# Layer 2 of a fused convolution and two-layer MLP kernel starts after three chunks of layer 1 in place of two

## The chip, the cores and the metric

One core of a Trainium2 chip runs the whole kernel. The metric is the device time of one execution in microseconds (us), a median over several executions. The engines of the core work in parallel, each through its own queue in order: PE (TensorE, the matmuls; PEld is its loading of weights), DVE (VectorE), ACT (ScalarE), POOL (GpSimd), SP (SyncE, which only issues DMAs here).

## The reference

```python
w = softmax(weight_gen, axis=-1)                 # (2, 4096, 8 heads, 7 taps)
x1[b, s, h, g] = sum_k w[b, s, h, k] * xpad[b, s + k, h, g]   # 192 = 8 heads x 24, causal, 7 taps
x1 = x1.reshape(8192, 192)
x2 = (sigmoid(x1 @ w_gate) * (x1 @ w_val)) @ w_out       # layer 1, 192 -> 1536 -> 192
h  = x2 @ w_in
out = (h * cos(h)) @ w_out2                              # layer 2, 192 -> 2048 -> 192
```

The weights of both layers come as 64-bit floats and are decoded on the chip; the products are computed to more than one float32r by a split of each operand in a high and a low half.

## The kernel before, in words

The 8192 tokens are cut into 16 **chunks** of 512 tokens. For each chunk a **convolution** on DVE (7 multiplications by a tap, `tap`, of 128x768 elements, and sums of them) gives x1 with tokens on the partitions. PE transposes it (`transposes`, L335, tile `pt`) and ACT and DVE split it in high and low halves (`split_input`, L357 and L363), which makes the layer's input `xT`.

A **step** of a layer is one call of `hidden` (18 matmuls of 64x512, L413, into two of the four PSUM banks `ph`) and the work on its result. There are 12 steps in layer 1 of a chunk and 8 in layer 2. In layer 1 ACT takes the sigmoid (L515), DVE multiplies (L518, which frees the two banks), ACT and POOL make the halves `gh` (L556) and `gl` (L557), and PE makes 10 matmuls with them (`out_matmuls`, L432) some two steps later. A step of layer 2 has two such tiles, so 20 of these matmuls, and a cosine in place of the sigmoid. At the end of layer 1 of a chunk `finish1` adds up the sums on ACT and DVE (L441, L442) and makes the input of layer 2 with three instructions on POOL (L452 and twice L122). At the end of layer 2 `finish2` transposes the result back (L469, tile `pf`) and stores it.

The order of the segments is written out by hand. Before the change it is layer 1 of chunks 0 and 1, then layer 2 of chunk 0, layer 1 of chunk 2, layer 2 of chunk 1, layer 1 of chunk 3, and so on: `LEAD = 2` segments of layer 1 first. Each engine's order of work follows from the order in which the loop over `steps` writes it. Side work is put at named steps by the list `side` (a step from which it may come, a step at which it must, a cost; `do_side`): the softmax of a group of chunks, the taps of the next chunk, and the **decoding** of weights. Decoding one unit takes ACT (L110, L113, for the weights into layer 2 also L147), DVE (L115), ACT (L120) and POOL (L122 for a unit of `w_in`, twice L184 for a unit of an output matrix). The eight units of layer 2 (four of `w_in`, four of `w_out2`) are decoded while layer 1 of chunk 1 runs, at steps 1 + i * 11 // 8.

For chunks 0, 1 and 2 the seven products of the taps are not added on DVE. `conv_products` keeps them, and PE transposes all seven into the same PSUM tile, which adds them up there: 112 small matmuls in place of 16. From chunk 3 on `conv_ops` adds them on DVE (L309): 7 multiplications and 6 additions, and 16 transposes. The transposes of a chunk stand in the last step of the layer 1 segment before its own.

The input tiles live in three buffers: `xB` for every layer 1 but chunk 0's, `xA` and `xC` in turn for layer 2.

## Time and profile before

| | us |
|---|---|
| median of 3 executions (1251.09 to 1253.61) | 1252.81 |
| the profiled execution | 1251.61 |
| its span in the trace | 1249.8 |
| PE busy | 1219.4 (98%) |
| DVE busy | 902.1 (72%) |
| ACT busy | 792.8 (63%) |
| POOL busy | 713.0 (57%) |

A share of busy time is a mean over the whole span. The table of stretches shows where an engine is full: in a row, an engine whose busy time equals the length of the stretch never rests in it. A row of the timeline gives start and length of some instructions that stand together, and in brackets how long the engine sat idle before them and what ended that. Where one instruction of a kind takes longer than the others of its shape, it waited inside itself for something that the profile doesn't name.

### The profile page before, as it was taken

To read this page: it belongs to the slowest core of one execution; us is meant where nothing else is said; L and a number is where in the kernel's file an instruction comes from. 1 tells how busy PE (TensorE), PEld (TensorE's weight loads), DVE (VectorE), ACT (ScalarE), POOL (GpSimd) and SP (SyncE) were. 2 spreads that over 40 slices of the span, in tenths; PEclk is the share of its full clock that TensorE was granted. 3 is DMA by queue.
4 is the path that set the end of the run, shared out by engine and by line. 5 is a ranking of instruction groups with operands and counts; after the bars stand their busy time and mean duration, and the time that the engine had idled before them with its cause. 6 is when DMAs were issued, how large, how long until landed. Compare 5 with 4: busy or idle time off the path is not lost.

```text
span 1249.8 us, 26898 instructions
## 1 busy us (share of the span) xinstructions
PE 1219.4 (98%) x11056; PEld 1058.3 (85%) x11056; DVE 902.1 (72%) x1309; ACT 792.8 (63%) x1326; POOL 713.0 (57%) x531
## 2 busy tenths in 40 slices
PE   6889999999999999999999999999999999999997
PEld 5677988898898888888898888989889899888886
DVE  7967887777877676877667787775877767683585
ACT  6765856648475574857557485664847557484674
POOL 3958645647465474655637465463746546464563
PEclk8999999999999999999999999999999999999999
DMA  9902202121111211111121120112111121020010
GB/s 250 248 20 58 63 14 69 27 70 27 45 32 34 69 26 54 43 45 27 26 82 27 46 52 14 58 27 74 27 45 26 40 58 26 14 52 14 1 27 26
DMA packets 27403, 61.94 MB, mean 50 GB/s; under 512 B 2580, under 2 KB 7698, under 8 KB 27280
## 3 DMA queue, kind: packets, MB, share of 16 engines
q1 hardware_dynamic: 26368, 59.09, 17.5%
q8 instruction: 86, 1.41, 0.5%
q10 hardware_dynamic: 912, 1.13, 0.3%
q14 instruction: 37, 0.30, 0.1%
HBM read 30.33 MB, written 6.29 MB: 29 GB/s over the span
## 4 chain that ended last, share of the span: by engine, by line
PE 84%; DVE 1%; ACT 1%; issue 0%; DVEq 0%; ACTq 0%
PE ph L413 46%; PE po L432 36%; PE pf L469 1%; PE pt L335 1%; DVE wk L546 0%; ACT wk L542 0%; ACT gh L556 0%; DVE wk L529 0%; DVE wk L532 0%; DVE wk L518 0%; ACT va L441 0%; DVE wk L537 0%; DVE gl L557 0%; ACT wk L536 0%; DVE pr L283 0%
## 5 line engine op out<-in xcount | busy, mean ns | idle before, releaser
L557 POOL TENSOR_TENSOR gl<-wk,gh 128x512 fp32r<-128x512 f32 x446 | 607.0, 1367 | 498.5 <-ACT gh L556 381.3
L413 PE MATMUL ph<-xT,unit 64*128 64x512 f32 x5760 | 772.8, 390 | 8.5 <-DVE wk L518 4.6
L413 PEld LDWEIGHTS ph<-xT,unit 64*128 64x128 f32 x5760 | 617.9, 185 | 104.0 <-DVE wk L518 13.6
L432 PE MATMUL po<-gh,outu 64*128 64x512 f32 x2688 | 552.1, 390 | 2.2 <-ACT gh L556 1.8
L432 PE MATMUL po<-gl,outu 64*128 64x512 f32 x1792 | 467.7, 389 | 4.6 <-POOL gl L557 4.6
L556 ACT ACTIVATE gh<-wk 128x512 fp32r<-128x512 f32 (+1 forms) x450 | 283.1, 629 | 249.1 <-DVE wk L518 206.1
L432 PEld LDWEIGHTS po<-gh,outu 64*128 64x128 f32 x2688 | 405.5, 185 | 37.2 <-ACT gh L556 2.7
L432 PEld LDWEIGHTS po<-gl,outu 64*128 64x128 f32 x1792 | 315.7, 185 | 28.8 <-POOL gl L557 6.4
L518 DVE TENSOR_TENSOR wk<-ph,wk 128x512 f32<-128x512 f32 x192 | 131.7, 686 | 146.4 <-ACT wk L515 136.0
L546 DVE SCALAR_TENSOR_TENSOR wk<-ph,wk 128x512 f32<-128x512 f32 (+1 forms) x258 | 168.4, 687 | 42.5 <-ACT wk L542 42.5
L542 ACT ACTIVATE wk<-wk,sin_bias 128x512 f32<-128x512 f32 (+1 forms) x258 | 173.0, 714 | 19.4 <-DVE wk L532 8.8
L515 ACT ACTIVATE wk<-ph 128x512 f32<-128x512 f32 x192 | 113.6, 592 | 57.8 <-PE ph L413 56.9
L529 DVE TENSOR_SCALAR wk<-ph 128x512 f32<-128x512 f32 x129 | 88.0, 682 | 64.1 <-PE ph L413 62.3
L536 ACT ACTIVATE wk<-ph 128x512 int32<-128x512 f32 x129 | 75.5, 585 | 73.6 <-PE ph L413 73.0
L309 DVE TENSOR_TENSOR acc<-acc,pr 128x768 f32<-128x768 f32 x78 | 102.0, 1308 | 0.4
L283 DVE TENSOR_TENSOR pr<-xp,sm 128x768 f32<-128x768 f32 x84 | 96.0, 1144 | 0.0
L532 DVE SCALAR_TENSOR_TENSOR wk<-wk,ph 128x512 f32<-128x512 f32 x129 | 88.1, 683 | 4.4
L537 DVE TENSOR_TENSOR wk<-wk,ph 128x512 f32<-128x512 int32 x129 | 87.3, 677 | 0.0
L442 DVE TENSOR_TENSOR va<-po,va 128x512 f32<-128x512 f32 x32 | 22.0, 688 | 39.1 <-PE po L432 29.1
L363 DVE TENSOR_TENSOR xT<-pt,xT 64x256 fp32r<-64x256 f32 (+1 forms) x76 | 27.2, 413 | 21.5 <-ACT xT L357 21.3
L357 ACT ACTIVATE xT<-pt 64x256 fp32r<-64x256 f32 (+1 forms) x66 | 20.4, 378 | 21.5 <-PE pt L335 21.3
L122 POOL TENSOR_TENSOR unit<-wf,unit 128x768 fp32r<-128x768 f32 (+1 forms) x11 | 22.2, 2022 | 15.8 <-ACT unit L120 15.8
(61 smaller groups left out, 507.8 us busy)
## 6 DMA issues: line engine op xcount, KB each, us to landing
xT<-xT SPq DMA_DIRECT2D x90, 256.0 KB, 3.9
xp<-in_x_dram SPq DMA_DIRECT2D x13, 960.0 KB, 4.8
out_dram<-o SPq DMA_DIRECT2D x16, 384.0 KB, 2.3
rawo<-in_moe_w_out_dram SPq DMA_DIRECT2D x7, 768.0 KB, 15.9
raw<-in_moe_w_in_dram SPq DMA_DIRECT2D x8, 384.0 KB, 15.7
raw<-in_moe_w_gate_dram SPq DMA_DIRECT2D x5, 384.0 KB, 12.8
raw<-in_moe_w_val_dram SPq DMA_DIRECT2D x4, 384.0 KB, 15.3
sm<-in_weight_gen_dram SPq DMA_DIRECT2D x3, 336.0 KB, 5.1
```

Source lines behind the costliest of these rows:

```text
L283: nc.vector.tensor_tensor(out=out.rearrange("p t (h g) -> p t h g", g=G), in0=xp[c][:, k:k + TC, :].rearrange("p t (h g) -> p t h g", g=G) ...
L309: nc.vector.tensor_tensor(out=acc, in0=acc, in1=last, op=ALU.add)
L413: nc.tensor.matmul(ps[i], lhsT=u.t[r, w, (s + i) % NQ, c0:c0 + P], rhs=xt[r, x, s, :], start=n == 0, stop=n == len(terms) - 1,)
L432: nc.tensor.matmul(po[2 * i + a], lhsT=w[r, d0:d0 + P], rhs=g[r], start=first and g is gh and d0 < D, stop=last and g is gl,)
L515: nc.scalar.activation(out=self.w[0], in_=self.ps[0], func=AF.Sigmoid)
L518: nc.vector.tensor_tensor(out=self.w[0], in0=self.ps[1], in1=self.w[0], op=ALU.mult)
L529: nc.vector.tensor_scalar(out=w, in0=u, scalar1=0.25, scalar2=ROUND_MAGIC, op0=ALU.add, op1=ALU.add)
L532: nc.vector.scalar_tensor_tensor(out=w, in0=w, scalar=ROUND_MAGIC, in1=u, op0=ALU.subtract, op1=ALU.subtract)
L542: nc.scalar.activation(out=w, in_=w, func=AF.Sin, scale=-SIN_SCALE, bias=sin_bias)
L546: nc.vector.scalar_tensor_tensor(out=w, in0=self.ps[i][:, r], scalar=TWO_PI, in1=w, op0=ALU.mult, op1=ALU.mult)
L556: nc.scalar.activation(out=gh, in_=w, func=AF.Copy)
L557: eng.tensor_tensor(out=gl, in0=w, in1=gh.bitcast(F32), op=ALU.subtract)
```

## The change

- The segments become layer 1 of chunks 0, 1 and 2, then layer 2 of chunks 0 and 1, then layer 1 of chunk 3, layer 2 of chunk 2, layer 1 of chunk 4, and so on.
- Chunk 2 uses `conv_ops` as the later chunks do: its seven products are added on DVE, and PE transposes one tile.
- The eight units of layer 2's weights are decoded over layer 1 of chunks 1 and 2, at steps 1 + i * 22 // 8.
- The transposes and the split for chunk 3 move into step 5 of layer 2 of chunk 1, since no layer 1 segment stands right before chunk 3's own.
- The softmax group of chunks 3 to 5 becomes one of chunk 3 alone, loaded into the tile of the group before, and the groups of three start at chunk 4.
- The three input buffers take turns, for both layers.

```diff
-    groups = [(0, TC), (TC, 3 * TC)] + [(t0, min(t0 + GT, T)) for t0 in range(3 * TC, T, GT)]
+    groups = [(0, TC), (TC, 3 * TC), (3 * TC, 4 * TC)] + [(t0, min(t0 + GT, T)) for t0 in range(4 * TC, T, GT)]
...
+    HOME = {(1, 0): "xA", (1, 1): "xB", (1, 2): "xA", (2, 0): "xC", (2, 1): "xB", (2, 2): "xA"}
+
+    def input_tile(layer, c):
+
+        tag = HOME.get((layer, c)) or ("xC", "xB", "xA")[c % 3]
+        return tpool.tile([P, 2, NQ, N], F32R, name="xT", tag=tag)
...
-        big = tpool.tile([P, K - 3, TC, D], F32, name="prs", tag="xA" if c == LEAD else "xB")
+        big = tpool.tile([P, K - 3, TC, D], F32, name="prs", tag="xB")
...
-    LEAD = 2
-    segments = [(1, c) for c in range(LEAD)]
-    for c in range(NCH):
+    LEAD = 3
+    FINAL = 4
+    segments = [(1, c) for c in range(LEAD)] + [(2, 0)]
+    for c in range(1, NCH):
         segments.append((2, c))
-        if c + LEAD < NCH:
-            segments.append((1, c + LEAD))
+        if c + 2 < NCH:
+            segments.append((1, c + 2))
...
-        todo[n1:] = [(seg_start[1, 1] + 1 + i * (J1 - 1) // 8, u) for i, (_, u) in enumerate(todo[n1:])]
+        todo[n1:] = [(seg_start[1, 1] + 1 + i * (2 * J1 - 2) // 8, u) for i, (_, u) in enumerate(todo[n1:])]
...
-                a, b = [(seg_start[1, c - 3], seg_start[1, c - 2]), (k0, k0)][group_at[c] == 2]
+                a, b = [(seg_start[1, c - 3], seg_start[1, c - 2]), (k0, k0)][group_at[c] in (2, 3)]
                 if a == b:
+                    a += group_at[c] == 2
                     at = [a - 1] * 2 * n + [a] + [a + 1] * n + [a + 2] * (n + 1)
...
-            if c <= LEAD:
-                n, ops = K, conv_products(c)
-                last = seg_start[1, c - 1] + J1 - 2
-                if c == LEAD:
-                    k0, k1 = k0 + 1, k1 + 2
-                at = [k1 + i * (last - k1) // n for i in range(n)] if c == LEAD else TAPS0
+            if c == 1:
+                n, ops, at = K, conv_products(c), TAPS0
...
-        inputs = {seg_start[1, c - 1] + J1 - (1 if c > 1 else AHEAD): c for c in range(1, NCH)}
+        inputs = {seg_start[1, c - 1] + J1 - (1 if c > 1 else AHEAD): c for c in range(1, NCH) if c != LEAD}
+        inputs[seg_start[2, 1] + FINAL + 1] = LEAD
...
+                if k in inputs:
+                    c1 = inputs[k]
+                    ops = transpose_ops(att[c1], c1)
+                    next(ops)
                 st.reduce(ended and ended.finish)
...
+                for _ in ops or ():
+                    pass
```

The first place is POOL's queue in layer 1 of chunk 1, from its step 2 on: `unit` and `outu` are decoded weights, `vc` and `xT` belong to `finish1` of chunk 0, `gl` are the low halves of the steps. Before:

```order
L122 TENSOR_TENSOR unit<-wf,unit 128x768
L557 TENSOR_TENSOR gl<-wk,gh 128x512
L184 TENSOR_TENSOR outu<-wf,outu 128x4x64
L184 TENSOR_TENSOR outu<-wf,outu 128x4x128
L452 TENSOR_TENSOR vc<-vc,vs 64x512
L557 TENSOR_TENSOR gl<-wk,gh 128x512
L122 TENSOR_TENSOR unit<-wf,unit 128x768
L122 TENSOR_TENSOR xT<-va,xT 128x512
L557 TENSOR_TENSOR gl<-wk,gh 128x512
L122 TENSOR_TENSOR xT<-vc,xT 64x512
L557 TENSOR_TENSOR gl<-wk,gh 128x512
L184 TENSOR_TENSOR outu<-wf,outu 128x4x64
```

The same place of POOL's queue in the changed kernel, from the same unit on:

```order
L122 TENSOR_TENSOR unit<-wf,unit 128x768
L567 TENSOR_TENSOR gl<-wk,gh 128x512
L462 TENSOR_TENSOR vc<-vc,vs 64x512
L567 TENSOR_TENSOR gl<-wk,gh 128x512
L184 TENSOR_TENSOR outu<-wf,outu 128x4x64
L184 TENSOR_TENSOR outu<-wf,outu 128x4x128
L122 TENSOR_TENSOR xT<-va,xT 128x512
L567 TENSOR_TENSOR gl<-wk,gh 128x512
L122 TENSOR_TENSOR xT<-vc,xT 64x512
L567 TENSOR_TENSOR gl<-wk,gh 128x512 x2
L122 TENSOR_TENSOR unit<-wf,unit 128x768
L567 TENSOR_TENSOR gl<-wk,gh 128x512 x3
```

Between the first unit and the end of that segment POOL had three units, four pairs of `outu`, the three instructions of `finish1` and nine `gl`; now it has two units and two pairs with the same three and nine, and one unit and two pairs follow in layer 1 of chunk 2.

The second place is DVE's queue in the same segment, after the sums of `finish1`: `prs`, `pr` and `acc` from `xp,sm` are taps, `wf` is a decoding, `wk<-ph,wk` frees the banks. Before:

```order
L115 SCALAR_TENSOR_TENSOR wf<-wf,rawo 128x768
L518 TENSOR_TENSOR wk<-ph,wk 128x512
L115 SCALAR_TENSOR_TENSOR wf<-wf,raw 128x768
L283 TENSOR_TENSOR prs<-xp,sm 128x768
L518 TENSOR_TENSOR wk<-ph,wk 128x512
L283 TENSOR_TENSOR prs<-xp,sm 128x768
L518 TENSOR_TENSOR wk<-ph,wk 128x512
L115 SCALAR_TENSOR_TENSOR wf<-wf,rawo 128x768
L283 TENSOR_TENSOR prs<-xp,sm 128x768
L518 TENSOR_TENSOR wk<-ph,wk 128x512
L115 SCALAR_TENSOR_TENSOR wf<-wf,raw 128x768
L283 TENSOR_TENSOR prs<-xp,sm 128x768
```

The same place of DVE's queue in the changed kernel, where `acc<-acc,pr` is an addition of chunk 2:

```order
L528 TENSOR_TENSOR wk<-ph,wk 128x512
L286 TENSOR_TENSOR pr<-xp,sm 128x768
L312 TENSOR_TENSOR acc<-acc,pr 128x768
L528 TENSOR_TENSOR wk<-ph,wk 128x512
L115 SCALAR_TENSOR_TENSOR wf<-wf,rawo 128x768
L286 TENSOR_TENSOR pr<-xp,sm 128x768
L312 TENSOR_TENSOR acc<-acc,pr 128x768
L528 TENSOR_TENSOR wk<-ph,wk 128x512 x2
L286 TENSOR_TENSOR pr<-xp,sm 128x768
L312 TENSOR_TENSOR acc<-acc,pr 128x768
L528 TENSOR_TENSOR wk<-ph,wk 128x512
L115 SCALAR_TENSOR_TENSOR wf<-wf,raw 128x768
```

From those sums to the end of the segment DVE had seven taps and six decodings, 13 instructions; now it has eleven taps and additions and three decodings, 14. Layer 1 of chunk 2 then gets thirteen taps and additions of chunk 3, three decodings and two instructions of a softmax.

The third place is PE's queue around the transposes of chunk 3, first before, in the last step of layer 1 of chunk 2 (`po` are the sums of the output matmuls):

```order
L432 MATMUL po_2262<-gl,outu 128x512
L432 MATMUL po_2264<-gl,outu 128x512
L335 MATMUL pt<-ident,acc 128x64 x2
L335 MATMUL pt<-ident,acc 64x64 x8
L335 MATMUL pt<-ident,acc 128x64 x6
L432 MATMUL po_2261<-gh,outu 128x512
L432 MATMUL po_2263<-gh,outu 128x512
L432 MATMUL po_2261<-gh,outu 128x512
```

And in the changed kernel, in step 5 of layer 2 of chunk 1:

```order
L442 MATMUL po_2677<-gh,outu 128x512
L442 MATMUL po_2675<-gl,outu 128x512
L442 MATMUL po_2677<-gl,outu 128x512
L345 MATMUL pt<-ident,acc 128x64 x2
L345 MATMUL pt<-ident,acc 64x64 x8
L345 MATMUL pt<-ident,acc 128x64 x6
L423 MATMUL ph<-xT,unit 128x512 x18
L442 MATMUL po_2674<-gh,outu 128x512
```

Before, 20 output matmuls stood between the transposes and the next `hidden`; now the next `hidden` follows at once.

## Rows read from the trace of the kernel before

**Rows 1.** The page's first part: busy time, share and instructions of each engine.

```profile
PE 1219.4 (98%) x11056; PEld 1058.3 (85%) x11056; DVE 902.1 (72%) x1309; ACT 792.8 (63%) x1326; POOL 713.0 (57%) x531
```

**Rows 2.** Stretches: length, busy us (instructions) of PE, PEld, DVE, ACT, POOL; clock, DMA.

```profile
76.40:117.90 41.50, 35.06 (x262) 26.31 (x260) 31.20 (x26) 29.48 (x46) 34.96 (x23) 0.96 0.15 44
...
168.10:206.00 37.90, 37.83 (x348) 32.14 (x346) 30.02 (x41) 17.86 (x32) 17.66 (x12) 1.00 0.22 67
```

**Rows 3.** Timeline of PE, layer 1 of chunk 1: start, us, line, instructions.

```profile
76.41 2.41 PE L413 MATMUL ph<-xT,unit 64*128 64x512 f32 x18
...
90.05 0.79 PE L432 MATMUL po<-gl,outu 64*128 64x512 f32 x2 [3.08 <-POOL gl L557]
...
111.57 2.42 PE L413 MATMUL ph<-xT,unit 64*128 64x512 f32 x18
...
114.74 2.42 PE L413 MATMUL ph<-xT,unit 64*128 64x512 f32 x18
```

**Rows 4.** Stretches after that stall, columns as in rows 2.

```profile
90.00:92.00 2.00, 1.95 (x10) 1.56 (x12) 2.00 (x1) 0.99 (x2) 2.00 (x2) 0.50 0.00 0
92.00:94.00 2.00, 2.00 (x16) 1.58 (x13) 2.00 (x1) 0.00 (x0) 2.00 (x2) 0.65 0.00 0
```

**Rows 5.** Instructions by line, 76.4 to 117.9: shortest/median/longest ns.

```profile
L557 POOL TENSOR_TENSOR gl<-wk,gh x9: 1262/1307/2010, 81.4 to 117.5; 128x512 fp32r<-128x512 f32 x9
L122 POOL TENSOR_TENSOR unit<-wf,unit x3: 1822/1827/2487, 78.3 to 104.5; 128x768 fp32r<-128x768 f32 x3
L184 POOL TENSOR_TENSOR outu<-wf,outu x8: 730/1418/2053, 84.2 to 116.3; 128x256 fp32r<-128x256 f32 x4, 128x512 fp32r<-128x512 f32 x4
```

**Rows 6.** Busy DVE in that stretch: first the taps (L283), then the decodings (L115).

```profile
76.40:117.90 41.50, 17.83 (x7) 0.96 0.15 44
76.40:117.90 41.50, 6.46 (x6) 0.96 0.15 44
```

**Rows 7.** Timeline of DVE and POOL at three places.

```profile
88.92 6.16 DVE L283 TENSOR_TENSOR prs<-xp,sm 128x768 f32<-128x768 f32 x1
...
169.00 1.29 POOL L557 TENSOR_TENSOR gl<-wk,gh 128x512 fp32r<-128x512 f32 x1 [2.32 <-ACT gh L556]
...
181.24 0.94 DVE L309 TENSOR_TENSOR acc<-acc,pr 128x768 f32<-128x768 f32 x1
181.25 2.08 POOL L557 TENSOR_TENSOR gl<-wk,gh 128x512 fp32r<-128x512 f32 x1 [3.09 <-ACT gh L556]
```

**Rows 8.** Timeline of PE: transposes of chunk 2, then of chunk 3.

```profile
117.92 2.14 PE L335 MATMUL pt<-ident,prs 64*128 64x64 f32 x62
...
123.66 2.36 PE L413 MATMUL ph<-xT,unit 64*128 64x512 f32 x18
...
196.25 0.69 PE L335 MATMUL pt<-ident,acc 64*128 64x64 f32 x13
...
199.15 2.35 PE L413 MATMUL ph<-xT,unit 64*128 64x512 f32 x18
```

**Rows 9.** Timeline of PE: `hidden` before and after `pf`, layer 1, then layer 2.

```profile
171.34 2.78 PE L413 MATMUL ph<-xT,unit 64*128 64x512 f32 x18
...
179.22 4.46 PE L413 MATMUL ph<-xT,unit 64*128 64x512 f32 x36
...
1207.56 2.42 PE L413 MATMUL ph<-xT,unit 64*128 64x512 f32 x18
...
1211.87 2.42 PE L413 MATMUL ph<-xT,unit 64*128 64x512 f32 x18
...
1217.64 2.75 PE L413 MATMUL ph<-xT,unit 64*128 64x512 f32 x17 [0.59 <-DVE wk L546]
...
1222.48 0.39 PE L413 MATMUL ph<-xT,unit 64*128 64x512 f32 x1
```

**Rows 10.** Groups by line, whole span: ACT's table for Exp; a split's subtraction.

```profile
L363 DVE TENSOR_TENSOR xT<-pt,xT 128x256 fp32r<-128x256 f32 x32 | 12.1, 420 | 21.4 <-ACT xT L357 21.3
...
L242 ACT ACT_TABLE_LOAD x5 | 6.4, 1283 | 0.1
```

More of the change, by code (lines that the diff above doesn't have):

```diff
@@ L216, in load_group @@
         t0, t1 = groups[g]
-        pool = fpool if tag == "wf" else opool
-        s = pool.tile([P, (t1 - t0) * H, K], F32, name="sm", tag=tag)
+        if g == 2:
+            s, b0 = sm[groups[1][0]]
+        else:
+            pool = fpool if tag == "wf" else opool
+            s, b0 = pool.tile([P, (GT if g == 1 else t1 - t0) * H, K], F32, name="sm", tag=tag), t0
         cuts = sorted({t0, t1, min(max(t0, T - ROT), t1)})
@@ L374, in transpose_ops @@
             transposes(p, src, n == 0, n == len(srcs) - 1)
-        xt = xT[1, c] = tpool.tile([P, 2, NQ, N], F32R, name="xT", tag="xB")
+        xt = xT[1, c] = input_tile(1, c)
         yield
-        yield from split_input(xt, p, c < LEAD)
+        yield from split_input(xt, p, c < 2)
     def split_input(xt, p, fast):
@@ L686, in dyn_conv_glu_cos_mlp @@
                 add_side(at, at, [cost(TC * H * K)] * len(at), softmax_ops(group_at[c]))
[L687 to L692 removed]
+            if c == 1:
+                n, ops, at = K, conv_products(c), TAPS0
             else:
                 n, ops = 2 * K, conv_ops(c)
[L695 removed]
+                k0 = at = [seg_start[1, c - 1] + j for j, m in enumerate(TAPS[group_at.get(c) in (2, 3)]) for _ in range(m)]
             add_side(k0, at, [cost(TC * D)] * n, ops)
@@ L803, in dyn_conv_glu_cos_mlp @@
                 load_x(c + 2)
-                if c + 4 in group_at and group_at[c + 4] > 2:
+                if c + 4 in group_at and group_at[c + 4] > 3:
                     load_group(group_at[c + 4], "wf")
+            if layer == 1 and c == 0 and j == J1 - 2:
+                load_group(2, "o")
             if layer == 2 and c == 0 and j == 5:
-                load_group(2, "wf")
+                load_group(3, "wf")
         for q in waiting:
```

13 lines of the change are left out of this document (6 added, 7 removed).

## The prediction, made before the run

> **What bounds the kernel now.** I read the busy times first: PE is busy for 98% of the span [rows 1], so only what PE does without need, and the little time in which it waits, can be won. I read the stretches next. In a later layer 1 segment, 168 to 206 us, PE rests for 0.07 of 37.9 us [rows 2], although DVE is busy for 30 of them. In layer 1 of chunk 1, 76.4 to 117.9 us, PE is busy for only 35.1 of 41.5 us, at a mean granted clock of 0.96, and POOL is busy for 35.0 [rows 2]. This is the stretch that the change touches.
>
> What would the stretch last if PE never waited? One step of layer 1 takes 114.74 - 111.57 = 3.17 us [rows 3]. From the `hidden` at 76.41 to the transposes at 117.92 [rows 3, 8] there are steps 2 to 11, so 31.7 us. The stretch took 41.5: **9.8 us lost**. The largest single stall is 3.08 us for a `gl` of POOL [rows 3]. Behind it the granted clock falls to its lower level, 1.2 GHz (0.50 for two microseconds, then a mean of 0.65) [rows 4], which costs 2 x 0.50 + 2 x 0.35 = 1.7 us, a part of the 9.8.
>
> Why is POOL late? Its instructions without hindrance take 1.26 us for a `gl` and 1.82 for a unit [rows 5]; the two for an output unit take 0.73 and 1.42. The three of `finish1` have as many columns as a `gl`, and I take 1.26 each. So 9 x 1.26 + 3 x 1.82 + 4 x 2.15 + 3.8 = 29.2 us. But a `gl` that starts together with an addition on DVE takes 2.08 us in place of 1.29 [rows 7], 0.79 more, and a tap on DVE that starts behind POOL's queue takes 6.16 us [rows 7]. Both have all operands in SBUF; they run one after the other, not side by side. With 13 such instructions on DVE [rows 6] this makes 29.2 + 13 x 0.79 = 39.5 of the 41.5 us. What I see is one shared thing that is full, and POOL and DVE queue for it. On DVE the instruction that frees the PSUM banks stands behind the waiting tap, and PE behind that; on POOL a `gl` stands behind a unit, and PE's output matmuls behind it.
>
> The Trainium skill (SBUF — State Buffer, "Who interferes with whom") calls it an exclusive lock: a VectorE instruction with two SBUF inputs and a GpSimd instruction that reads SBUF block each other for the whole instruction. The trace agrees on the exclusion, but its price is 0.79 us, not the whole 0.94 [rows 7]. With 0.94 for each and nothing of the lateness absorbed the two segments would lose 4.6 and 3.2 us in the sum below, which then ends at 1249.8 us in place of 1246.5; the measured row decides.
>
> **The change part by part.**
>
> *Transposes of chunk 2.* From the first transpose to the next `hidden` 123.66 - 117.92 = 5.74 us go by with 112 transposes, and 199.15 - 196.25 = 2.90 with 16 [rows 8], the same 20 output matmuls in both. PE works without a pause there, so 96 fewer save **2.84 us**. The six additions that take their place are counted next.
>
> *Layer 1 of chunk 1, steps 2 to 11.* By the order of instructions POOL loses one unit and two pairs: 29.2 - 1.82 - 4.30 = 23.1 us. DVE has 14 instructions in place of 13. The sum of the shared thing is 23.1 + 14 x 0.79 = 34.1 us, against 31.7 of PE: 2.4 too much, where before it was 39.5 - 31.7 = 7.8. Bounds: nothing is lost if 2.4 us of lateness fits in what `gl` and banks may be late; by the difference of the sums alone, 9.8 - (39.5 - 34.1) = 4.4 us are lost. I take the ratio of before, 2.4 x 9.8 / 7.8 = **3.0 lost**, which lies between them.
>
> *Layer 1 of chunk 2.* PE needs 12 x 3.17 + 0.63 = 38.7 us. (The 28 matmuls of a step take 3.17, so 20 take 2.27, and 2.90 - 2.27 = 0.63 are the 16 transposes.) POOL has 12 `gl`, one unit, two pairs and `finish1`: 15.1 + 1.8 + 4.3 + 3.8 = 25.0. DVE has 13 taps and additions, 3 decodings and 2 of the softmax, at 0.79 each 14.2. Sum 39.2: 0.5 too much, where this segment lost nothing before. Lower bound 0 lost. Upper bound: DVE needs as long for each as it did in the full stretch, (17.83 + 6.46) / 13 = 1.87 us [rows 6], so 18 x 1.87 = 33.7; its other work was 31.2 - 24.3 = 6.9 us in ten steps [rows 2, 6], 8.3 in twelve, and the four subtractions of a split are 4 x 0.42 = 1.7 [rows 10]. That makes 43.7, 5.0 more than PE. I take **1.5**, near the low end, since the sums nearly meet. In it is a burst on ACT in the first steps: the softmax's Exp moves one step into the segment, and brings two loads of a table at 1.28 us [rows 10] ahead of a sigmoid; the two banks in reserve cover most of that.
>
> *Layer 2 of chunk 1, right behind layer 2 of chunk 0.* Two layer 2 segments stand in a row at the end of the kernel already. The `pf` transposes there take 1222.48 - 1211.87 = 10.61 us for two steps, where two steps of 1211.87 - 1207.56 = 4.31 and 0.63 make 9.25: 1.36 lost, with a wait for DVE's last product of the step [rows 9]. In layer 1 the same is 179.22 - 171.34 = 7.88 against 6.97: 0.91 lost [rows 9]. Moving one `pf` costs 0.45. The transposes of chunk 3 move to step 5; they take two banks just as `pf` does, and the 20 output matmuls that covered them [rows 8] now stand ahead of them. No row shows this; I take the nearest, 1.36. Below 0 it can't be, since in layer 1 they cost no wait; above, twice as much, 2.72, as the split's eight instructions on ACT and DVE stand ahead of the next step's. Together **1.8 lost**, 0.45 to 3.2.
>
> *Edits at nothing.* The buffers in turn: each is free a whole segment before it is written. The loads of chunk 3's softmax weights move behind the load of chunk 2's inputs on SP; the DMA queues are nearly idle from 66 us on, and no tap of chunk 3 comes before step 3 of chunk 2's segment. If the cover fails, the first tap waits and up to 1 us is lost. One change of ACT's tables between the layers falls away and one for the Exp is added.
>
> **The sum**, against the profiled execution: -2.84 - 9.8 + 3.0 + 1.5 + 1.8 = -6.3. The span of 1249.8 becomes 1243.5 and the execution of 1251.6 us 1245.3; as the median of the runs is 1.2 above that execution, 1252.8 becomes **1246.5 us**.
>
> **The rivals.**
>
> *The stalls vanish.* 2.4 and 0.5 us too much fit in the reserve of banks and of steps that wait for their output matmuls. Then -2.84 - 9.8 + 1.8 = -10.8: 1242.0. For it: the segment at 168 us holds 12 `gl` and DVE at 30 of 37.9 without loss [rows 2]. Against: the two segments come one after the other, and lateness adds up.
>
> *The stalls only spread.* DVE keeps its slow pace of 1.87 us through both segments: 4.4 + 5.0 + 1.8 = 11.2 lost in place of 9.8, less 2.84, is -1.4: 1251.4. For it: the moved decodings meet thirteen taps and additions of chunk 3, and chunk 2's additions come on top. Against: POOL's share falls by a quarter, and POOL set the pace. The lock for whole instructions, which the Trainium skill states on the page named above, would end between this and my forecast, by the figure given there.
>
> *Slower.* The burst on ACT in the first three steps of chunk 2's segment (a decoding, two table loads, the sums, a second decoding) falls on DVE's slow pace, PE stalls there once as at 90 us, and the clock falls: 3.08 + 1.7 = 4.8 on top of the last case, 1256.2. [...]
>
> *It doesn't do what it says:* the order shows 16 transposes for chunk 2 and the spread decodings, so I give this nothing.
>
> **How the numbers follow.** Forecast 0.55, stalls vanish 0.15, stalls spread 0.20, slower 0.10. A measurement can tell about 0.2%, 2.5 us, from no change. Forecast and vanished stalls are faster by more, 0.70; spread stalls are the same, 0.20; the last is slower, 0.10. The range reaches from the vanished stalls, 1242.0, to the spread ones, 1251.4, and half a microsecond beyond either end.
>
> **What would show it.** Right: one short group of transposes before chunk 2's layer 1; no wait of PE for a `gl` above 2 us; PE's granted clock at 1.00 in layer 1 of chunks 1 and 2; the two segments some 4 to 5 us longer than their steps; a wait for DVE's product after each of `pf` and `pt` in layer 2 of chunk 1. Wrong: taps of 2 us and more throughout chunk 2's segment with PE waiting for the multiplication that frees its banks, or a sigmoid that comes some 3 us late behind the table loads.

## The result, and the profile after

The changed kernel is slower by 1.0%: 1264.63 us (median of 4 executions, 1263.81 to 1265.69) against 1251.99 us of the kernel before on the same chip (also 4), a ratio of 1.0101 (95% interval 1.0089 to 1.0113). The forecast was 1246.5 us, with 1251.9 as the upper end; it missed by 18 us and in sign. The profiled execution took 1264.97 us, its span is 1263.1 us.

The page's first part, which answers [rows 1]:

```profile
PE 1223.8 (97%) x10960; PEld 1047.2 (83%) x10960; DVE 915.1 (72%) x1315; ACT 791.9 (63%) x1325; POOL 718.2 (57%) x531
```

PE has 96 instructions fewer (the transposes of six products) and is busy 4.4 us longer: it does less, in part at a lower clock. The stretches of the changed kernel answer [rows 2]; the columns are the same. They are layer 1 of chunk 1 from step 2 on, the transposes of chunk 2, step 0 of chunk 2's layer 1, and its steps 1 to 11:

```profile
76.12:115.29 39.17, 34.24 (x263) 27.43 (x260) 31.63 (x26) 23.54 (x38) 30.81 (x20) 0.91 0.16 46
115.29:118.19 2.90, 2.90 (x39) 2.89 (x37) 1.81 (x5) 1.77 (x6) 1.23 (x2) 1.00 0.00 0
118.19:128.57 10.38, 5.90 (x31) 4.04 (x29) 3.17 (x5) 3.72 (x5) 2.29 (x1) 0.67 0.32 76
128.57:170.35 41.78, 36.36 (x291) 28.27 (x288) 32.11 (x32) 21.18 (x34) 27.62 (x19) 0.96 0.15 44
```

How long would they be without a wait? A later run (`e17`) held steps 1 to 11 of chunk 2's layer 1 at 32.64 us, with PE busy all the time and the granted clock at 1.00. These are 11 x 18 matmuls into `ph`, and 10 output matmuls in nine of the steps (by `OUTS`, steps 6 and 8 have none): 288, so 0.1133 us each. Steps 2 to 11 have 260, so 29.5 us. Then chunk 1's steps lost 12.0 us before (41.5, [rows 2]) and lose 9.7 now; step 0 of chunk 2 loses 10.38 - 3.17 = 7.2, and steps 1 to 11 lose 9.1. From step 2 of chunk 1 to step 4 of chunk 3 the kernel before takes 170.18 us and the changed one 182.46: 12.3 of the 13.3 us by which the spans differ.

PE's waits over the whole span (total, times, longest, in us) name three of the causes:

```profile
PE ph L423 <- DVE wk L528: 9.5, 10, 3.4
...
PE po L442 <- POOL gl L567: 5.2, 5, 3.2
PE ph L423 <- DMA xT<-xT: 4.5, 1, 4.5
```

The last of them stands at the head of chunk 2's layer 1, on PE's timeline:

```profile
118.19 0.52 PE L423 MATMUL ph<-xT,unit 64*128 64x512 f32 x2
123.18 4.40 PE L423 MATMUL ph<-xT,unit 64*128 64x512 f32 x16 [4.48 <-DMA xT<-xT]
```

PE begins with the half of `xT` that is there, then waits 4.48 us for the other half, which `exchange` copies by DMA. The 16 matmuls behind it take 4.40 us in place of some 2.2, at the lower clock. The split of chunk 2 takes this slow form in both kernels, but before a whole segment of layer 2 stood between split and use, and now none. The call said `c < LEAD` before, with `LEAD = 2`; the change raised `LEAD` to 3 and wrote `c < 2` in its place, a line that the excerpt of the diff above leaves out, and so it kept the slow form.

The first cause, in chunk 1 (DVE, then POOL, then PE):

```profile
83.95 2.05 DVE L286 TENSOR_TENSOR pr<-xp,sm 128x768 f32<-128x768 f32 x1
85.93 5.17 DVE L312 TENSOR_TENSOR acc<-acc,pr 128x768 f32<-128x768 f32 x1
91.03 0.68 DVE L528 TENSOR_TENSOR wk<-ph,wk 128x512 f32<-128x512 f32 x1
```

```profile
83.17 2.02 POOL L462 TENSOR_TENSOR vc<-vc,vs 64x512 f32<-64x512 f32 x1
85.15 2.00 POOL L567 TENSOR_TENSOR gl<-wk,gh 128x512 fp32r<-128x512 f32 x1
87.12 1.95 POOL L184 TENSOR_TENSOR outu<-wf,outu 128x256 fp32r<-128x256 f32 x2
89.04 1.25 POOL L122 TENSOR_TENSOR xT<-va,xT 128x512 fp32r<-128x512 f32 x1
```

```profile
88.01 0.39 PE L423 MATMUL ph<-xT,unit 64*128 64x512 f32 x1
91.76 4.20 PE L423 MATMUL ph<-xT,unit 64*128 64x512 f32 x17 [3.37 <-DVE wk L528]
```

An addition of chunk 2's sum starts at 85.93 and ends when POOL has gone through a `gl`, an output unit's pair and an `xT` without a pause: 5.17 us for what takes 0.94 alone [rows 7]. The multiplication that frees a PSUM bank stands behind it on DVE, PE waits 3.37 us, and the next 17 matmuls take 4.20 us at the lower clock. It is the stall of [rows 3] over again, with DVE in POOL's place.

The second cause, a `gl` that comes 3.24 us late, stands in chunk 2's steps (POOL, then DVE, then PE):

```profile
138.97 2.14 POOL L184 TENSOR_TENSOR outu<-wf,outu 128x256 fp32r<-128x256 f32 x2 [1.51 <-ACT outu L120]
141.07 1.97 POOL L462 TENSOR_TENSOR vc<-vc,vs 64x512 f32<-64x512 f32 x1
143.00 1.98 POOL L567 TENSOR_TENSOR gl<-wk,gh 128x512 fp32r<-128x512 f32 x1
```

```profile
139.99 1.94 DVE L286 TENSOR_TENSOR acc<-xp,sm 128x768 f32<-128x768 f32 x1
141.85 2.01 DVE L286 TENSOR_TENSOR pr<-xp,sm 128x768 f32<-128x768 f32 x1
```

```profile
145.04 0.79 PE L442 MATMUL po<-gl,outu 64*128 64x512 f32 x2 [3.24 <-POOL gl L567]
```

The `gl` stands behind a decoding's pair and `finish1`'s addition `vc`, and two taps of chunk 3 fall into the same 4 us: `vc` and `gl` take 1.97 and 1.98 us each, where 1.27 and 1.26 is what they take without a tap beside them (`e15`, below).

### The profile page after: what moved, and what is told of

It reads as the page before. It is cut to its first block, busy times and chain, and to the rows that moved or that the text cites. A ratio compares the mean times of both kernels' runs of the same rounds, so it can differ in the third digit from the quotient of the medians.

```text
span 1263.1 us, 26717 instructions
## 1 busy us (share of the span) xinstructions
PE 1223.8 (97%) x10960; PEld 1047.2 (83%) x10960; DVE 915.1 (72%) x1315; ACT 791.9 (63%) x1325; POOL 718.2 (57%) x531
## 4 chain that ended last, share of the span: by engine, by line
PE 77%; DVE 1%; ACT 1%; issue 0%; DVEq 0%; ACTq 0%
PE ph L423 43%; PE po L442 33%; PE pf L479 1%; PE pt L345 1%; DVE wk L556 0%; ACT wk L552 0%; ACT gh L566 0%; DVE wk L539 0%; DVE wk L542 0%; DVE wk L528 0%; ACT vc L451 0%; DVE wk L547 0%; DVE gl L567 0%; ACT wk L546 0%; DVE pr L286 0%
## 5 line engine op out<-in xcount | busy, mean ns | idle before, releaser
L312 DVE TENSOR_TENSOR acc<-acc,pr 128x768 f32<-128x768 f32 x84 | 116.7, 1390 | 0.4
L286 DVE TENSOR_TENSOR pr<-xp,sm 128x768 f32<-128x768 f32 x88 | 102.7, 1168 | 0.0
L547 DVE TENSOR_TENSOR wk<-wk,ph 128x512 f32<-128x512 int32 x129 | 87.3, 677 | 0.0
```

The source lines that it names most:

```text
L286: nc.vector.tensor_tensor(out=out.rearrange("p t (h g) -> p t h g", g=G), in0=xp[c][:, k:k + TC, :].rearrange("p t (h g) -> p t h g", g=G) ...
L312: nc.vector.tensor_tensor(out=acc, in0=acc, in1=last, op=ALU.add)
```

## Experiments

Theory A: the head's DMA has lost its cover. Theory B: DVE's instructions with two SBUF operands and POOL's take turns, and PE's banks and `gl` stand behind them. Theory C came up on the way: the Exp and its two table loads on ACT. The runs were taken on several chips, so each ratio is to the kernel before on the same chip. The stretches of the runs, by the starts of `hidden` on PE's timeline ("chunk 1" is steps 2 to 11 with the transposes of chunk 2; "pair" goes from layer 2 of chunk 0 to the start of step 3 of chunk 3's layer 1; all in us):

| run | chunk 1 | head | steps 1-11 | pair | median us | ratio to before (95%) |
|---|---|---|---|---|---|---|
| changed kernel | 42.1 | 10.4 | 41.8 | 85.0 | 1264.63 | 1.0089-1.0113 |
| e1_fast2 | 42.1 | 5.4 | 45.2 | 85.0 | 1263.46 | 1.007-1.01 |
| e2_products2 | 43.8 | 9.8 | 41.7 | 85.0 | 1265.87 | 1.0088-1.0121 |
| e3_decode1 | 48.8 | 10.2 | 37.9 | 85.0 | 1266.81 | 1.0095-1.0125 |
| e6_onetap | 34.7 | 10.0 | 38.4 | 85.0 | 1254.56 | 1.0006-1.0025 |
| e9_nopool_decode | 38.8 | 10.4 | 41.6 | 85.0 | 1261.66 | 1.0058-1.0092 |
| e7_sums_later | 42.1 | 5.4 | 40.4 | 87.3 | 1261.62 | 1.0056-1.0086 |
| e10_both_later | 42.1 | 5.4 | 39.1 | 92.0 | 1263.22 | 1.0069-1.0099 |
| e14_space | 40.6 | 10.8 | 42.1 | 85.0 | 1264.73 | 1.008-1.0113 |
| e11_exp_early | 42.1 | 5.4 | 39.1 | 84.9 | 1259.74 | 1.0048-1.0078 |
| e12_exp_space | 40.6 | 5.5 | 40.1 | 85.0 | 1259.72 | 1.0046-1.0076 |
| e13_exp_space_ahead | 45.7 together | | 39.9 | 85.0 | 1258.34 | 1.0036-1.0066 |
| e15_exp_onetap | 34.7 | 5.3 | 37.4 | 85.0 | 1249.64 | 0.9974-0.9992 |
| e17_all_sums_later | 45.7 together | | 32.6 | 86.8 | 1252.84 | 1.0-1.0019 |
| e19_ten_four | 45.7 together | | 34.1 | 85.0 | 1251.56 | 0.998-0.9998 |

**The head (theory A).**

```diff
-        yield from split_input(xt, p, c < 2)
+        yield from split_input(xt, p, c < LEAD)
```

> Theory A: the largest part of the 12.6 us is the wait at the head of chunk 2's layer 1, where the input's other halves come by a DMA that a whole layer 2 segment covered before. Making them by ACT and DVE straight from PSUM, as for chunks 0 and 1, takes the DMA out: step 0 falls from 10.4 us to 5 or 6 (it still waits some 2 us for ten subtractions on DVE), the clock stays at full level there, and the time goes to 1259 to 1261 us. Theory B: POOL and DVE, which exclude each other, are behind their work anyway, and the wait only stands where their backlog would stop PE a moment later: the steps behind lose what step 0 gains, and the time stays above 1263.

Measured: the head fell to 5.4 us as theory A says, which shows that the DMA made the wait. The time fell by only 1.2 us (2.0 by the ratios) and stayed above 1263, as theory B expected, since steps 1 to 11 lasted 3.4 us longer. There a new stall had come up, which neither theory names; first on PE, then ACT, which it waited for:

```profile
128.64 2.58 PE L423 MATMUL ph<-xT,unit 64*128 64x512 f32 x18
133.71 1.94 PE L442 MATMUL po<-gh,outu 64*128 64x512 f32 x4 [2.49 <-ACT va L451]
135.03 1.05 PE L442 MATMUL po<-gl,outu 64*128 64x512 f32 x2
```

```profile
129.58 1.28 ACT L245 ACT_TABLE_LOAD   x1
130.87 0.39 ACT L245 ACTIVATE sm<-sm 128x224 f32<-128x224 f32 x1
131.28 1.28 ACT L525 ACT_TABLE_LOAD   x1
132.57 0.60 ACT L525 ACTIVATE wk<-ph 128x512 f32<-128x512 f32 x1
133.07 0.59 ACT L451 ACTIVATE va<-po 128x512 f32<-128x512 f32 x1
```

PE wants to begin the next sum in `po`, whose copy to `va` stands on ACT behind 2.95 us of Exp and table loads. In the changed kernel the same burst, at 129.4 us, cost next to nothing: PE began step 2 3.1 us later there, at 131.77 us, after its wait at the head. Taking one lateness away uncovered the next. Theory C.

**The transposes and the sums.** `e2` gives chunk 2 its seven products and 112 transposes back; `e4` is the kernel before with chunk 2's sums on DVE.

```diff
@@ e2, on the changed kernel (the buffer of its products left out)
-            if c == 1:
+            if c <= 2:
                 n, ops, at = K, conv_products(c), TAPS0
+                if c == 2:
+                    last = seg_start[1, 1] + J1 - 2
+                    k0, k1 = k0 + 1, k1 + 2
+                    at = [k1 + i * (last - k1) // n for i in range(n)]
@@ e4, on the kernel before
-            if c <= LEAD:
+            if c < LEAD:
```

> The changed kernel with chunk 2's seven products transposed on PE as before (six additions fewer on DVE, 96 transposes more, 2.84 us of PE). Theory B: six additions less at 0.79 us of the shared time make layer 1 of chunk 1 lose some 5 us in place of 9.7, which more than pays the transposes: 1262 to 1263 us. Theory A alone: the additions cost nothing, and the time is 2.8 longer, 1267.

> The kernel before with one part of the change alone: chunk 2's products are added on DVE. Theory B: six additions in a segment in which POOL and DVE are already behind cost 4 to 6 us, against 2.84 us of transposes saved: 1253 to 1255 us. Theory A alone (and the prediction's first term): the saving comes through, 1249 us.

Measured: `e2` with the products took 1265.87 us, between the two theories; chunk 1's steps shrank by 1.1 us, not by 5, and the transposes grew by 2.84. In the kernel before, the sums made chunk 1's steps 1.6 us longer and the transposes 2.84 shorter; 1251.81 us, a ratio of 0.9997 (0.9988 to 1.0007), again between the two. So 2.84 us is right to the digit, and six additions in that stretch give 1.1 to 1.6 of it back: a price of 0.79 us for each, 4.7 in all, is too much here.

**Where the decodings stand.** `e3` puts the decodings back into chunk 1 alone. `e14` spreads them over both chunks, but not between the three instructions of `finish1`:

```diff
@@ e3
-        todo[n1:] = [(seg_start[1, 1] + 1 + i * (2 * J1 - 2) // 8, u) for ...]
+        todo[n1:] = [(seg_start[1, 1] + 1 + i * (J1 - 1) // 8, u) for ...]
@@ e14
+        todo[n1:] = [(seg_start[1, 1] + d, u) for d, (_, u) in zip((1, 5, 7, 9, 12, 17, 20, 22), todo[n1:])]
```

> The changed kernel with all eight units decoded in layer 1 of chunk 1 again. Theory B, what counts is the sum of POOL's and DVE's work over both segments: layer 1 of chunk 1 loses 5 to 6 us more, steps 1 to 11 of chunk 2's 5 to 6 less, and the time stays within 2 us of 1264.6. Rival: in chunk 2's segment the decodings are not what is late, so it keeps its 9.2 us and the time rises to 1269 or more.

> The changed kernel, with the decodings of layer 2's weights put at other steps: in layer 1 of chunk 1 at steps 1, 5, 7 and 9 in place of 1, 3, 6 and 9, in that of chunk 2 at 0, 5 and 8 in place of 0, 2 and 5. The same work, but none of it stands on GpSimd between finish1's subtractions, which come in steps 2 to 5. Theory B in a sharper form (an addition on VectorE gets no turn as long as GpSimd has ready instructions in a row: at 85.93 us one took 5.17 us, until gl, the output unit's pair and the xT were through): the stall of 3.4 us in chunk 1 goes, its steps 2 to 11 fall from 39.2 to 34.5 to 37 us, chunk 2's steps 1 to 11 from 41.8 to 39 to 42, and the time is 1258 to 1262. Rival (the sum of both engines' work decides, not its order): 38 to 40 us, and the time stays at 1263 to 1266.

Measured: `e3` moved the loss, 6.7 us more in chunk 1 and 3.9 fewer in chunk 2, and at 1266.81 us it lay 2.2 above the changed kernel (1.1 by the ratios), about where theory B put it and below the rival. `e14` took 1.5 us from chunk 1 (37.7 for its steps, just above the range; the largest stall there fell from 3.37 to 2.12 us) and won nothing in all, 1264.73 us, which is the rival's time: the pair that now stood at step 5 of chunk 2 came behind a `gl`, an addition on DVE took 3.94 us there, and PE waited 3.84. The sharper form of theory B didn't hold as a remedy: a `gl` and a pair are enough for such a wait.

**Work left out (theory B).** `e6` leaves out twelve of the taps and additions for chunks 2 and 3 each, `e9` POOL's subtractions in the decoding of layer 2's weights, in whose place ACT writes zeros.

```diff
@@ e6, in conv_ops
         tap(c, 0, acc)
+        if c in (2, 3):
+            return
@@ e9, in Unit.halves; alike in OutUnit.halves
-            split(u[:, 0:NQ * W], u[:, NQ * W:], f)
+            if self in units2:
+                nc.scalar.activation(out=u[:, 0:NQ * W], in_=f, func=AF.Copy)
+                nc.scalar.activation(out=u[:, NQ * W:], in_=f, func=AF.Copy, scale=0.0)
```

> The changed kernel, with the convolution sums of chunks 2 and 3 cut down to their first tap: six taps and six additions of VectorE are left out for each of the two chunks, so these two chunks of the output hold other values. Nothing of GpSimd's work is touched. Theory B (VectorE's operations with two SBUF operands and GpSimd's wait for each other, and the banks of the PE wait behind both): layer 1 of chunk 1, steps 2 to 11, falls from 39.2 to 30 to 32 us, steps 1 to 11 of chunk 2 from 41.8 to 33.5 to 35, gl on GpSimd goes back from 1.80 and 1.57 to about 1.3 us, and the time falls by 13 to 17 us to 1248 to 1251. The head of chunk 2's layer 1 (10.4 us) stays, since nothing of it is touched (theory A: it is the DMA of the slow split). Rival: GpSimd is late by its own work alone. Then chunk 1's steps keep more than half of their loss, 35 us or more.

> The changed kernel, with GpSimd's subtractions left out where the weights of layer 2 are decoded: ScalarE writes zeros in their place, so layer 2 is computed with rounded weights. VectorE keeps all its work; GpSimd loses two units and two pairs in layer 1 of chunk 1 and one unit and two pairs in that of chunk 2 (8 and 6 us). Theory B: the two losses shrink by about as much as GpSimd's work, chunk 1's steps 2 to 11 to 32 to 35 us and chunk 2's steps 1 to 11 to 35 to 38 us, the time to 1252 to 1257; VectorE's taps stay near 1.5 us only where they meet a gl. Rival: VectorE alone is full, with its 13 to 14 slow operations. Then chunk 1's steps stay above 37 us and the time above 1260.

Measured for `e6`: chunk 1's steps fell from 39.2 to 31.9 us, 2.4 above 29.5, and POOL's `gl` from 1.80 to 1.29 us, though nothing of POOL's work was touched. First the changed kernel, then `e6` (busy us, mean ns of one, idle time before it):

```profile
L567 POOL TENSOR_TENSOR gl<-wk,gh 128x512 fp32r<-128x512 f32 x11 | 19.8, 1804 | 5.7 <-ACT gh L566 5.7
```

```profile
L569 POOL TENSOR_TENSOR gl<-wk,gh 128x512 fp32r<-128x512 f32 x10 | 12.8, 1292 | 2.9 <-ACT gh L568 2.9
```

So in chunk 1 it is DVE's sums, through POOL and through DVE's own queue, that make most of the loss. For chunk 2 it missed: 33.5 to 35 us were expected and 38.4 came, and the time was 1254.56 us, not 1248 to 1251. `e9` took 3.3 us from chunk 1, less than the 4 to 7 expected, and nothing from steps 1 to 11 of chunk 2; its time, 1261.66 us, is the rival's. It isn't a clean run, as the zeros give ACT 2.9 us more work in chunk 1's steps (busy 26.4 in place of 23.5), in which PE now waited for ACT, 0.8 and 0.7 us. So neither the sums nor the decodings alone explain chunk 2's steps.

**The sums and decodings of chunk 2's segment, later.** Both on top of `e1`: `e7` does half of chunk 3's sums in layer 2 of chunk 0 (with the load of chunk 4's inputs behind them); `e10` moves decodings there too, on top of `e7`.

```diff
@@ e7 and e10
+            if c == LEAD:
+                k0 = at = [seg_start[1, 2] + j for j in (3, 5, 6, 7, 8, 9, 10)] + [s2 + j for j in range(7)]
             add_side(k0, at, [cost(TC * D)] * n, ops)
@@ e10
+        todo[-3:] = [(s2 + d, u) for d, (_, u) in zip((0, 1, 3), todo[-3:])]
```

> The changed kernel with two edits: chunk 2's split is the one without the DMA (as run alone before), and the second half of chunk 3's taps and additions, seven operations of VectorE, is done in layer 2 of chunk 0 and not in layer 1 of chunk 2. Theories A and B together: the head of chunk 2's layer 1 stays at 5.4 us, its steps 1 to 11 fall from 45.2 to 38 to 41 us, layer 2 of chunk 0 grows by 0 to 1 us, and the time is 1257 to 1260. Rival: the loss of these steps comes from the lateness that they inherit, or from ScalarE's loads of the Exp table; then they stay above 43 us and the time at 1262 to 1264.

> The kernel with chunk 2's split without the DMA and chunk 3's sums half in layer 2 of chunk 0, and besides the last three decodings of layer 2's weights (one unit and two output units, 6.1 us of GpSimd) moved from layer 1 of chunk 2 to the first steps of layer 2 of chunk 0. Theory B: steps 1 to 11 of chunk 2 fall to 34 to 37 us, layer 2 of chunk 0 grows by 0.5 to 3 us (GpSimd has 1.7 us to spare in each of its steps), and the time is 1253 to 1257, the kernel before at best. Rival: layer 2 of chunk 0 has no room, since GpSimd's gl there are late too; then it grows by what chunk 2's segment loses and the time stays within 1.5 us of that with the sums alone moved.

Measured: `e7` won 4.8 us in steps 1 to 11 and lost 2.3 in layer 2, more than the 0 to 1 expected; so its time, 1261.62 us, came out above the range. In `e10` only two output units moved, 4.3 us of POOL and not 6.1 as the text above says. They won 1.4 more and cost 4.7 in layer 2, where they stood among the `gl` around `finish1` of chunk 2: 1263.22 us, 1.6 above `e7`. That was the rival, and a little worse. And in both the stall of 2.5 us for `va`, behind the Exp, stayed.

**The Exp (theory C), and all together.** `e11` does chunk 3's softmax together with that of chunks 1 and 2 at the start; `e12` adds `e14`'s places for the decodings, `e13` the transposes of chunk 2 one step earlier; `e15` is `e11` with the taps of `e6` left out.

```diff
@@ e11, e12, e13 and e15, with e1's split (places of the softmax's parts left out)
-    groups = [(0, TC), (TC, 3 * TC), (3 * TC, 4 * TC)] + [...]
+    groups = [(0, TC), (TC, 4 * TC)] + [...]
@@ e13
-        inputs = {seg_start[1, c - 1] + J1 - (1 if c > 1 else AHEAD): c for ...}
+        inputs = {seg_start[1, c - 1] + J1 - (1 if c > 2 else AHEAD): c for ...}
```

> The changed kernel with two edits: chunk 2's split is the one without the DMA, and chunk 3's softmax is done together with that of chunks 1 and 2 at the start (one load of 12 steps of weights, one Exp), so that no Exp and no load of its table stands in layer 1 of chunk 2. Theory C: the two table loads on ScalarE (1.28 us each, with the Exp 2.95 us) hold up finish1's copies and the sigmoid, PE waits 2.5 us and the clock falls. Then steps 1 to 11 of chunk 2 fall from the 45.2 us of the run with the split alone to 37 to 40 us; the start grows by 0 to 1.3 us; the time is 1256 to 1259.5. Rival (theory B alone, VectorE and GpSimd are full): they stay above 43 us and the time at 1262 to 1265.

> All three edits: the split without the DMA, chunk 3's softmax at the start, the decodings of layer 2's weights put apart from finish1's subtractions. Theories A, B and C together: chunk 1's steps 2 to 11 35 to 37 us, the head of chunk 2 5.4, its steps 1 to 11 35 to 38, and the time 1252 to 1256, about the kernel before. Rival (the losses of the two segments are one sum that only moves): no better than the run without the third edit by more than 1 us.

> The same with the transposes of chunk 2 one step earlier, as those of chunk 1 have been all along, so that the split has a step's matmuls of layer 1 of chunk 1 as cover. Then the head of chunk 2's layer 1 falls from 5.4 to 3.2 to 4 us; the last addition of chunk 2's sums must be done a step earlier, which can cost up to 2 us on VectorE. The time is 1250 to 1256, and within 2 us of the run without it. Rival: VectorE isn't done with the sums by then and PE waits at the transposes for 2 us or more; then it is slower than the run without it.

> The kernel with the split without the DMA and chunk 3's softmax at the start, and with the sums of chunks 2 and 3 cut down to the first tap (twelve operations of VectorE left out for each of the two chunks, which get other values). If the loads for Exp and the sums are the whole loss of steps 1 to 11 of chunk 2, these fall to 32.6 to 34 us (from 39.1 with the sums and 38.4 with the loads), chunk 1's steps 2 to 11 to 32 us as in the first-tap run, and the time to 1246 to 1249. If the lateness comes from elsewhere, they stay above 35 us.

Measured: without the Exp, steps 1 to 11 fell from 45.2 to 39.1 us, which is in theory C's range, and the stall for `va` was gone; the time, 1259.74 us, lies 0.2 above the range. But `e11` changes a second thing, which its text doesn't name. With the softmax at the start, chunk 3's taps need not wait for it, and the kernel's list then spreads them over the whole segment. The first tap of chunk 3, in `e1`, then in `e11`:

```profile
140.23 1.93 DVE L286 TENSOR_TENSOR acc<-xp,sm 128x768 f32<-128x768 f32 x1
```

```profile
126.34 0.95 DVE L283 TENSOR_TENSOR acc<-xp,sm 128x768 f32<-128x768 f32 x1
```

How much of the 6.1 us is the Exp and how much the taps' new places, no run separates. `e12` won nothing more (1259.72 us, its rival): most of what it took from chunk 1 it lost in chunk 2. `e13` brought the head to 3.4 us as expected, but its time, 1258.34 us, is above the 1250 to 1256 of its text. And `e15`, with neither Exp nor sums, still took 37.4 us in steps 1 to 11 where 32.6 to 34 were expected. What was left in `e15`, on POOL and on PE:

```profile
129.81 1.99 POOL L184 TENSOR_TENSOR outu<-wf,outu 128x256 fp32r<-128x256 f32 x2 [1.50 <-ACT outu L120]
131.76 1.27 POOL L461 TENSOR_TENSOR vc<-vc,vs 64x512 f32<-64x512 f32 x1
132.99 1.26 POOL L566 TENSOR_TENSOR gl<-wk,gh 128x512 fp32r<-128x512 f32 x1
```

```profile
134.31 0.50 PE L441 MATMUL po<-gl,outu 64*128 64x512 f32 x2 [1.66 <-POOL gl L566]
134.65 0.50 PE L441 MATMUL po<-gh,outu 64*128 64x512 f32 x2
134.94 0.63 PE L441 MATMUL po<-gl,outu 64*128 64x512 f32 x2
135.37 3.54 PE L422 MATMUL ph<-xT,unit 64*128 64x512 f32 x18
```

A `gl` stands behind an output unit's pair and the addition of `finish1`, as in the changed kernel: a decoding in the wrong place, this time without DVE's doing, and half the stall. And in `e13`, where the decodings stand apart from `finish1` and the Exp is gone, an addition of chunk 3 waits behind a `gl` and a pair:

```profile
142.21 2.00 POOL L564 TENSOR_TENSOR gl<-wk,gh 128x512 fp32r<-128x512 f32 x1
144.17 1.93 POOL L184 TENSOR_TENSOR outu<-wf,outu 128x256 fp32r<-128x256 f32 x2
```

```profile
142.99 3.93 DVE L309 TENSOR_TENSOR acc<-acc,pr 128x768 f32<-128x768 f32 x1
```

```profile
147.58 4.20 PE L420 MATMUL ph<-xT,unit 64*128 64x512 f32 x17 [3.83 <-DVE wk L525]
```

So each run has another largest stall in chunk 2's steps: 3.24 us for a `gl` (changed kernel), 2.49 for `va` (`e1`), 2.54 for a `gl` (`e6`), 1.66 (`e15`), 3.83 for DVE (`e13`). Whichever stays, these steps are 4.8 (`e15`) to 12.5 us (`e1`) above 32.6, with the clock and smaller waits behind it. `e17` is `e13` with six of chunk 3's fourteen taps and additions moved to layer 2 of chunk 0, and the load of chunk 4's inputs behind them as in `e7`. `e19` moves four, and besides, to later steps, the two small multiplications that scale the softmax of chunks 2 and 3.

```diff
@@ e17
+                k0 = at = [seg_start[1, 2] + j for j in (0, 2, 3, 4, 6, 7, 9, 10)] + [s2 + j for j in (3, 3, 4, 5, 6, 7)]
@@ e19
+                k0 = at = [seg_start[1, 2] + j for j in (0, 2, 3, 3, 4, 6, 7, 8, 9, 10)] + [s2 + j for j in (4, 5, 6, 7)]
```

> The changed kernel with all edits: split without the DMA, transposes of chunk 2 a step earlier, softmax of chunk 3 at the start, decodings apart from finish1, and six of chunk 3's fourteen taps and additions in steps 3 to 7 of layer 2 of chunk 0. Steps 1 to 11 of chunk 2 from 39.9 to 35 to 38 us, layer 2 of chunk 0 0.5 to 2 us longer, the time 1254.5 to 1258. If it isn't below the kernel before, three chunks' layer 1 in a row don't pay with what was found.

> The same, and ten of chunk 3's fourteen taps and additions in layer 1 of chunk 2, four in layer 2 of chunk 0 (eight and six before). Layer 2 of chunk 0 gets 0.8 to 1.5 us shorter; chunk 2's steps 1 to 11 stay below 33.5 us if VectorE has room there, and the time is 1249.5 to 1251.5. Rival: two more are too many, and chunk 2's steps grow to 35 us or more.

Measured: in `e17` steps 1 to 11 have no wait any more, 39.9 to 32.6 us by this edit, more than was expected. Stretches of `e13`, then of `e17`:

```profile
124.95:164.88 39.93, 36.10 (x291) 29.85 (x288) 28.14 (x27) 20.51 (x35) 30.18 (x20) 0.91 0.16 46
```

```profile
124.87:157.51 32.64, 32.64 (x291) 27.94 (x289) 22.09 (x22) 20.84 (x35) 29.56 (x20) 1.00 0.11 26
```

The time, 1252.84 us, is some 11.5 us below the changed kernel's by the two ratios, and not below the kernel before. What is left is the part ahead: from step 2 of chunk 1 to the end of the head `e17` takes 45.7 us (52.4 in the changed kernel), where 29.5 + 2.9 + 3.2 = 35.6 would be without a wait, and step 2 of chunk 1 begins 3 us later (79.2 in place of 76.1). `e19` gives back 1.5 in these steps and wins 1.8 in layer 2: 1251.56 us, a ratio of 0.9989 to the kernel before. It is the only kernel that computes everything and whose whole interval lies below 1, by no more than 0.2%. Two more variants lie around it. `e18` is `e17` with those two multiplications late, `e20` is `e19` with the decodings of chunk 1 at steps 6, 8 and 10:

> The run with all edits, with the two multiplications that scale the softmax of chunks 2 and 3 taken out of layer 1 of chunk 0, where each took 1.4 to 1.5 us of VectorE, to its last step and to the last step of chunk 1's. If they made the late start, step 2 of chunk 1 begins 1 to 2 us earlier than at 79.2 us, and the time is 1250.5 to 1252. Rival: the start is late by the load and the two operations ahead of the first tap, 0.75 us, and by GpSimd; then it stays at 78.5 to 79.2 and the time at 1252 to 1253.5.

> The same, and the decodings in chunk 1's layer 1 at steps 1, 6, 8 and 10 in place of 1, 5, 7 and 9, so that the output unit's decoding stands a step behind finish1's last subtraction (at step 5 VectorE's operation took 3.23 us there and PE waited 2.1). Steps 2 to 11 get 0.5 to 2 us shorter, and the time is 1248 to 1251. Rival: the later decodings meet the transposes' split; then the head of chunk 2 grows by as much.

Measured: 1253.81 us (ratio 1.0 to 1.0018) and 1251.77 us (0.9985 to 1.0003), both slower than their ranges and neither clearly below the kernel before. In `e18` step 2 of chunk 1 began at 79.0 us, as in `e17`, but in that execution PE's clock had fallen in chunk 1's transposes, which took 3.47 us in place of 2.04 (last section). In `e19`, with the same two multiplications moved and 2.04 us there, it began at 77.65: so they seem to be 1.5 us of the late start, as expected, by one trace of each. Steps 1 to 11 took 33.9 us in `e18`, 1.3 more than in `e17`, which gave most of it back. In `e20` the stall of chunk 1 fell from 2.12 to 0.68 us and its steps by 1.6 us, and the stretch with the head stayed at 45.7 us: the head grew by as much, its rival.

**The lesson on the kernel before.** `e16` puts its decodings apart in the same manner: three of them into layer 2 of chunk 0.

```diff
@@ e16, on the kernel before
+        todo[n1:] = [(seg_start[1, 1] + d, u) for d, (_, u) in zip((1, 5, 7, 9, 15, 16, 17, 18), todo[n1:])]
```

> The kernel before, with the decodings of layer 2's weights at steps 1, 5, 7 and 9 of chunk 1's layer 1, and the last three (a unit and two output units, 6.1 us of GpSimd by the rows of before) in steps 3 to 5 of layer 2 of chunk 0. If GpSimd's decodings between finish1's subtractions and the sums make the loss there, steps 2 to 11 fall from 41.5 to 36 to 39 us, layer 2 of chunk 0 grows by 0 to 3 us, and the time is 1247 to 1252. Rival: layer 2 of chunk 0 gives it all back (there the run with both moved lost 7 us): 1252 to 1255.

Measured: chunk 1's steps fell from 41.5 to 34.7 us, with PE's clock at 1.00 in place of 0.96, and layer 2 of chunk 0 with the first three steps of the next segment grew from 44.4 to 53.0: 1253.9 us, 1.0014 (1.0005 to 1.0023). The rival. In the kernel before, that stretch has no idle PE, so what goes there has to be paid for (PE waited 4.5 us for `gl` there, in three waits).

## Why the prediction was wrong

*The sum.* From the forecast's -6.3 us to the measured +13.3 (spans 1249.8 and 1263.1) are 19.6 us. Layer 1 of chunk 2 is 14.9 of them, layer 1 of chunk 1 4.5; the other terms together are 0.3.

*Transposes of chunk 2:* right. 2.90 us, 2.84 saved; the order of matmuls is the same as in [rows 8].

*Layer 1 of chunk 1:* POOL and DVE do hinder each other there (`e6`), but the size was wrong twice. The stretch without a wait is 29.5 us, not 31.7: the step of 3.17 us [rows 3] was taken for every step, and two of ten have no output matmuls. And 9.7 us were lost, not 3.0 (7.5 by the prediction's own 31.7, above its upper bound of 4.4). The sum of both engines' work, 2.4 us over PE's, said little; `e4`'s six additions cost 1.6 us and not the 4.7 that the sum gives them. What costs most is a single wait of DVE behind several instructions of POOL (5.17 us): PE's 3.37 us and 2.5 at the lower clock behind it are 5.9 of the 9.7. 2.3 us were gained, not 6.8.

*Layer 1 of chunk 2:* this step failed. 1.5 us were forecast and 16.35 came. 7.21 of them are the head with the DMA of the slow split, which the prediction does not name at all (`e1` without that DMA takes 4.9 away; the rest is the fast split's own). Under "edits at nothing" it followed buffers, loads and tables, but not what the moved segment had left behind, the layer 2 of chunk 0 that covered `exchange`. 9.14 are steps 1 to 11. The upper bound, 5.0, let DVE take 1.87 us for each operation. The thirteen taps and additions took 1.56 us each there, and still nearly twice the bound was lost: a bound by DVE's pace holds neither the 3.24 us in which PE waits for a `gl` behind a pair and `vc`, nor the clock behind that wait (0.50 from 146 to 148 us). The burst on ACT was seen, and its cover by "two banks in reserve" was taken from the sigmoid's side; what it held up, in `e1`, was the copy of `po`. That the 9.14 come from these causes is shown by `e17`: with the fast split, and with the Exp, the decodings and six sums elsewhere, PE never rests in steps 1 to 11 (busy 32.64 of 32.64 us, clock 1.00). How the 9.14 divide among Exp, decodings and sums is open, since taking one away uncovers the next.

*Layer 2 of chunk 1 behind that of chunk 0:* about right, as a remainder. What is left of the 12.28 us is 12.28 + 2.84 + 2.34 - 16.35 = 1.1, where 1.8 were forecast.

*The rivals.* "Slower", 0.10 and 1256.2 us, came nearest. It had the right place and a stall with the clock behind it, and the second decoding of its burst is the pair ahead of the late `gl`. The table loads cost next to nothing in the changed kernel, and 2.49 us only in `e1`; without the Exp (`e11`) a wait of 2.40 us for a `gl` stayed. Its price was one stall on top of the spread ones, and there were three. The largest single term was in none of the cases.

*What would show it:* of the signs of right, the short group of transposes came; there was a wait for `gl` of 3.24 us, and the clock was 0.91 and 0.96 in the two segments. Of the signs of wrong, taps of 2 us came in part: five of the thirteen taps and additions in chunk 2's steps.

## What to carry to other kernels

When a segment is moved, list what each of its inputs waited behind, DMAs of its own making too: cover leaves with the segment that gave it. Add up busy time to see whether an engine is full, but look at the order of two engines that hinder each other: which instruction that PE needs stands behind a row of others. Where several such places lie in one segment, taking one away shows the next, so all have to go before the time moves far. A gain in a full stretch is real only when the stretch that takes the work has been looked at as closely.
